# A fused attention and MLP kernel whose instruction order is drawn from another simulation

## The chip, the cores and the metric

The kernel runs on one core of one Trainium2 chip. The metric is the time of one execution on the device, in microseconds (us). Before the change it is 1253.63 us, the median of three runs (1252.76 to 1253.79).

## What is computed

The reference is attention with normalised queries and keys, followed by two MLPs on the 1,792 tokens that come out of it:

```python
q_n, k_n = rmsnorm(q, g_q), rmsnorm(k, g_k)      # q, k, v: 4 x 12 x 448 x 64
attn = softmax(q_n @ k_n.T / 8)
x = (attn @ v), heads side by side               # 1792 x 768
x = (relu(x @ w_in) ** 2) @ w_out                # w_in 768 x 2048, w_out 2048 x 768
out = (((x @ w1) * (x @ w2)) @ w3) @ w_out2      # w1, w2 768 x 1024; w3 1024 x 1024; w_out2 1024 x 768
```

The MLP weights arrive as 64-bit words.

## The kernel before

There are 48 heads (4 batches of 12), and one loop (line 670) goes over them. Every product is made of values split into a high and a low part, so a matmul of the MLPs is three instructions in a row (`mm3`, lines 262 to 264).

**Attention of a head.** `head_prep` makes the scaled keys (`kx`, line 480, then `khl`, lines 108 and 114) and the queries `qh`, `ql`. `stage_k` transposes the keys (line 508). `stage_qk` runs twice per head and makes two score tiles each time (`sc`, lines 524 and 525), whose row maxima VectorE takes (line 526) and scales (line 527, `nb`); `stage_exp` has ScalarE make two tiles `p` from them (line 542). The score tiles have two PSUM buffers, so a pair of scores waits until ScalarE has read the pair before it. `stage_t` transposes `p` (line 564), ScalarE and VectorE split the result (`ptr`, `pte`), and `stage_v` multiplies with the values (line 616); line 605 transposes the sums. Every fourth head `group_prep` makes the norms of four more (lines 450 to 456, and `rsqrt`, lines 428 to 434).

**Fill.** Between the stages of a head, `fill` draws matmuls from a generator, so many for each stage. During heads 0 to 12 it is `gen_w3o`, which multiplies the two last weight matrices with each other (384 matmuls of 384 columns); from then on it is `gen_moe` of the batch that attention has just finished (448 columns). After the last head the MLPs of the last batch run alone.

**Weights.** A weight goes through a chain of units: SyncE loads 64-bit words (`raw64`, line 180, four buffers); ScalarE (line 194) and GpSimd or ScalarE (lines 200, 198) rework the two halves; VectorE joins them (line 207, `raw`, four buffers); ScalarE makes the high part and GpSimd or VectorE the low one (lines 106 and 114, `hl`, four buffers). Units of the first batch are also stored as 32-bit words, which later batches load. The 64-bit units are 120 in all: 32 for `gen_w3o` and 88 for the MLPs of the first batch. The profile's names leave out buffer numbers and write `raw` for `raw64` too, `x`, `act` and `x2` for the split operands of `mm3`.

**Order.** The kernel is traced as one program. When the `TileContext` closes, the framework's scheduler gives each engine its order: it plays the program in a simulation, and each time an engine is free there it takes, among the instructions that the simulation holds ready, the one that was traced first. On the chip each engine then keeps to that order, and semaphores make it wait.

## Time and profile before

| what | before |
|---|---|
| median of three runs | 1253.63 us |
| span of the profiled execution | 1246.1 us |
| TensorE matmul busy | 1173.5 us (94%), 6,192 matmuls |
| VectorE, ScalarE, GpSimd busy | 708.0, 728.9, 780.3 us |
| mean granted TensorE clock | 0.990 |

The span runs from the first to the last instruction. The profile lists no other time of that execution; the median is 7.5 us above its span.

### The profile page before, as it was taken

How to read it: one execution, taken by the hardware profiler on the slowest of the kernel's cores; microseconds unless marked ns; L12 is line 12 of the kernel's file. 1: busy time of each engine (PE TensorE's matmuls, PEld its weight loads, DVE VectorE, ACT ScalarE, POOL GpSimd, SP SyncE). 2: the span in 40 equal slices, each digit the busy share in tenths (PEclk: the TensorE clock that was granted, in tenths of full speed). 3: DMA queues.
4: the chain of work that ended last, by engine and by line, in shares of the span. 5: the costliest groups of instructions: out<-in, count | busy, mean ns of one | idle time of the engine just before them, and what ended most of it. 6: DMA issues, size and time to landing. Idle time of an engine off the chain costs nothing.

```text
span 1246.1 us, 18719 instructions
## 1 busy us (share of the span) xinstructions
PE 1173.5 (94%) x6192; PEld 1060.8 (85%) x6192; DVE 708.0 (57%) x1314; ACT 728.9 (58%) x1553; POOL 780.3 (63%) x772
## 2 busy tenths in 40 slices
PE   3789999898889899999999999999999999999998
PEld 2678888887777788999999999999999999999998
DVE  6699888867887775547567555655664421012110
ACT  5788876756655655566645555656645554443342
POOL 6775435645675665675776664755766556678773
PEclk9999999899999999999999999999999999999999
DMA  7774446876766655344333344332333333433342
GB/s 218 237 225 137 150 140 183 267 215 217 236 205 212 207 158 159 106 117 113 113 102 114 96 130 128 105 105 85 112 95 88 92 114 107 113 108 108 103 121 94
DMA packets 102129, 178.71 MB, mean 143 GB/s; under 512 B 11056, under 2 KB 65552, under 8 KB 102032
## 3 DMA queue, kind: packets, MB, share of 16 engines
q1 hardware_dynamic: 98576, 172.01, 46.6%
q10 hardware_dynamic: 3456, 5.51, 1.2%
q8 instruction: 49, 0.80, 0.3%
q14 instruction: 48, 0.39, 0.1%
HBM read 149.95 MB, written 27.53 MB: 142 GB/s over the span
## 4 chain that ended last, share of the span: by engine, by line
PE 69%; DVE 10%; DMA 7%; ACT 5%; POOL 5%; issue 4%; SPq 0%; ACTq 0%; DVEq 0%; POOLq 0%
PE mm L263 18%; PE mm L262 18%; PE mm L264 18%; PE pt L564 4%; PE kv L616 4%; POOL hl L114 2%; PE sc L524 2%; DMA raw<-w_in 2%; PE sc L525 2%; DVE raw L207 2%; DVE nb L526 2%; ACT p L542 2%; DMA kn<-k_nat 1%; DMA raw<-w 1%; ACT hl L106 1%
## 5 line engine op out<-in xcount | busy, mean ns | idle before, releaser
L114 POOL TENSOR_TENSOR hl<-raw,hl 128x384 fp32r<-128x384 f32 (+1 forms) x383 | 444.6, 1164 | 254.1 <-ACT hl L106 251.2
L106 ACT ACTIVATE hl<-raw 128x384 fp32r<-128x384 f32 (+1 forms) x416 | 233.2, 564 | 149.2 <-PE mm L264 82.2
L263 PE MATMUL mm<-x,hl 128*128 128x448 f32 (+1 forms) x832 | 306.4, 368 | 9.4 <-POOL x L114 9.4
L262 PE MATMUL mm<-x,hl 128*128 128x448 f32 (+1 forms) x832 | 311.0, 374 | 4.0 <-ACT x L106 1.8
L264 PE MATMUL mm<-x,hl 128*128 128x448 f32 (+1 forms) x832 | 305.5, 367 | 0.9 <-POOL hl L114 0.9
L262 PE MATMUL mm<-act,hl 128*128 128x448 f32 (+1 forms) x640 | 238.6, 373 | 0.0
L263 PE MATMUL mm<-act,hl 128*128 128x448 f32 (+1 forms) x640 | 235.8, 368 | 2.2 <-POOL act L114 1.7
L264 PE MATMUL mm<-act,hl 128*128 128x448 f32 (+1 forms) x640 | 234.7, 367 | 1.4 <-POOL hl L114 1.0
L542 ACT ACTIVATE p<-sc,nb,rr 112x448 f32<-112x448 f32 x192 | 137.3, 719 | 75.4 <-DVE nb L527 74.8
L263 PEld LDWEIGHTS mm<-x,hl 128*128 128x128 f32 x832 | 158.2, 190 | 23.2 <-POOL x L114 11.1
L262 PEld LDWEIGHTS mm<-x,hl 128*128 128x128 f32 x832 | 158.1, 190 | 18.9 <-ACT x L106 2.9
L264 PEld LDWEIGHTS mm<-x,hl 128*128 128x128 f32 x832 | 158.2, 190 | 14.9 <-POOL hl L114 2.0
L200 POOL TENSOR_SCALAR raw<-raw 128x384 uint32<-128x384 uint16 (+1 forms) x110 | 87.7, 798 | 84.6 <-DMA raw<-w_in 35.3
L526 DVE TENSOR_REDUCE nb<-sc 112x1 f32<-112x448 f32 x192 | 113.2, 616 | 37.7 <-PE sc L525 36.7
L263 PEld LDWEIGHTS mm<-act,hl 128*128 128x128 f32 x640 | 122.0, 191 | 12.9 <-POOL act L114 3.0
L264 PEld LDWEIGHTS mm<-act,hl 128*128 128x128 f32 x640 | 122.0, 191 | 11.8 <-POOL hl L114 1.8
L262 PEld LDWEIGHTS mm<-act,hl 128*128 128x128 f32 x640 | 122.2, 191 | 9.4 <-ACT act L106 0.2
L114 DVE TENSOR_TENSOR ptr<-pt,ptr 128x448 fp32r<-128x448 f32 x144 | 86.9, 618 | 69.8 <-ACT ptr L106 69.2
L207 DVE SCALAR_TENSOR_TENSOR raw<-raw 128x384 uint32<-128x384 uint32 (+1 forms) x120 | 85.5, 715 | 51.6 <-POOL hl L114 43.5
L564 PE MATMUL pt<-ident,p 112*128 112x112 f32 (+1 forms) x768 | 99.4, 265 | 12.6 <-DVE ptr L114 9.7
L194 ACT ACTIVATE raw<-raw 128x384 f32<-128x384 f32 (+1 forms) x120 | 71.1, 599 | 68.1 <-DMA raw<-w 25.0
L114 POOL TENSOR_TENSOR act<-gf,act 128x448 fp32r<-128x448 f32 x80 | 96.9, 1212 | 8.1 <-ACT act L106 3.2
(80 smaller groups left out, 1542.7 us busy)
## 6 DMA issues: line engine op xcount, KB each, us to landing
raw<-f_in SPq DMA_DIRECT2D x96, 192.0 KB, 2.4
raw<-f_out SPq DMA_DIRECT2D x72, 256.0 KB, 2.6
raw<-f SPq DMA_DIRECT2D x96, 192.0 KB, 2.4
raw<-w_in SPq DMA_DIRECT2D x32, 384.0 KB, 3.5
raw<-w_out SPq DMA_DIRECT2D x24, 512.0 KB, 4.5
raw<-w SPq DMA_DIRECT2D x32, 384.0 KB, 4.0
raw<-w3o SPq DMA_DIRECT2D x48, 256.0 KB, 2.7
qt<-q_t SPq DMA_DIRECT2D x48, 224.0 KB, 2.8
```

The lines of the kernel that those rows point to most:

```text
L106: nc.scalar.activation(out=out, in_=in_, func=AF.Copy)
L114: e.tensor_tensor(out=out, in0=in0, in1=in1, op=ALU.subtract)
L194: nc.scalar.activation(out=hi, in_=hi, func=AF.Prelu, scale=2.0**-112, alpha=-(2.0**32))
L200: nc.gpsimd.tensor_scalar(out=t[:, :n, 0], in0=low, scalar1=2.0**-13, scalar2=2.0**-14 - 0.5, op0=ALU.mult, op1=ALU.add)
L207: nc.vector.scalar_tensor_tensor(out=f[:, :n].bitcast(U32), in0=t[:, :n, 1], scalar=3, in1=t[:, :n, 0], op0=ALU.logical_shift_left, op1=AL ...
L262: nc.tensor.matmul(ps, w[:, 0, wk, :], x[0], start=(i == 0), stop=False)
L263: nc.tensor.matmul(ps, w[:, 0, wk, :], x[1], start=False, stop=False)
L264: nc.tensor.matmul(ps, w[:, 1, wk, :], x[0], start=False, stop=(i == last))
L526: nc.vector.tensor_reduce(out=nb[:, j:j + 1], in_=o[j], axis=AX.X, op=ALU.max, negate=True)
L542: nc.scalar.activation(out=p, in_=o[j], func=AF.Exp, scale=d["rq"][:, c:c + 1], bias=nb[:, j:j + 1], accum_out=sm[:, i, c:c + 1],)
L564: nc.tensor.transpose(ps[:kn, c * P:(c + 1) * P], d["p"][c][:, k0:k0 + kn], ident)
L616: nc.tensor.matmul(ps[:, :S], w, m, start=(n == 0), stop=(n == len(ops) - 1))
```

## The change

The context is told to schedule with the framework's timeline simulation. No instruction is added, removed or resized, and buffers and traced order stay; only the order in which each engine finds its instructions differs, and with it what each waits for.

```diff
-    with tile.TileContext(nc) as tc:
+    with tile.TileContext(nc, schedule_with_timeline_sim=True) as tc:
         attention_moe_kernel(tc, *args)
```

**GpSimd, the very start.** The keys of head 0 (`kx_149`, `khl_151`) and the first unit (`raw64_118`, which becomes `raw_243` and `hl_249`). Before:

```order
L480 TENSOR_TENSOR kx_149<-kn_113,rr_134 112x256
L200 TENSOR_SCALAR raw64_118<-raw64_118 128x512
L108 TENSOR_SCALAR khl_151<-kx_149 112x4x64
L114 TENSOR_TENSOR khl_151<-kx_149,khl_151 112x4x64
L200 TENSOR_SCALAR raw64_122<-raw64_122 128x384
```

Now:

```order
L200 TENSOR_SCALAR raw64_118<-raw64_118 128x512
L480 TENSOR_TENSOR kx_149<-kn_113,rr_134 112x256
L108 TENSOR_SCALAR khl_151<-kx_149 112x4x64
L114 TENSOR_TENSOR hl_249<-raw_243,hl_249 128x512
L114 TENSOR_TENSOR khl_151<-kx_149,khl_151 112x4x64
```

The first unit's work now stands ahead of the keys of head 0, twice. On VectorE the join of that unit (line 207, `raw_243`) likewise stands ahead of the last step of the first `rsqrt`, which `kx_149` needs.

**GpSimd, a little later.** The keys of heads 1 to 3 (`khl_199`, `khl_436`, `khl_651`) and the next units of the fill (`raw64_229` and `raw64_231`, split into `x_260`, `act_269`). Before:

```order
L480 TENSOR_TENSOR kx_197<-kn_113,rr_134 112x256
L108 TENSOR_SCALAR khl_199<-kx_197 112x4x64
L114 TENSOR_TENSOR khl_199<-kx_197,khl_199 112x4x64
L480 TENSOR_TENSOR kx_434<-kn_113,rr_134 112x256
L108 TENSOR_SCALAR khl_436<-kx_434 112x4x64
L114 TENSOR_TENSOR khl_436<-kx_434,khl_436 112x4x64
L480 TENSOR_TENSOR kx_649<-kn_113,rr_134 112x256
L108 TENSOR_SCALAR khl_651<-kx_649 112x4x64
L114 TENSOR_TENSOR khl_651<-kx_649,khl_651 112x4x64
L200 TENSOR_SCALAR raw64_229<-raw64_229 128x384
L200 TENSOR_SCALAR raw64_231<-raw64_231 128x384
```

Now:

```order
L200 TENSOR_SCALAR raw64_229<-raw64_229 128x384
L200 TENSOR_SCALAR raw64_231<-raw64_231 128x384
L114 TENSOR_TENSOR x_260<-raw_247,x_260 128x384
L114 TENSOR_TENSOR act_269<-raw_258,act_269 128x384
L480 TENSOR_TENSOR kx_197<-kn_113,rr_134 112x256
L108 TENSOR_SCALAR khl_199<-kx_197 112x4x64
L114 TENSOR_TENSOR khl_199<-kx_197,khl_199 112x4x64
L480 TENSOR_TENSOR kx_434<-kn_113,rr_134 112x256
L108 TENSOR_SCALAR khl_436<-kx_434 112x4x64
L200 TENSOR_SCALAR raw64_254<-raw64_254 128x384
```

Three heads' keys stood ahead of the units; now the units stand ahead of the keys.

**TensorE, head 10.** The first two scores of head 10 are `sc_1890` and `sc_1894`; `mm_1818` is a tile of `gen_w3o`, and `kv_2004` is the result of head 9. Before:

```order
L524 MATMUL sc_1890<-kt_1781,qh_1711 112x448
L525 MATMUL sc_1890<-kt_1781,ql_1712 112x448
L564 MATMUL pt_1920<-ident_103,p_1831 128x112
L564 MATMUL pt_1927<-ident_103,p_1737 128x112
L564 MATMUL pt_1927<-ident_103,p_1831 128x112
L524 MATMUL sc_1894<-kt_1781,qh_1711 112x448
L525 MATMUL sc_1894<-kt_1781,ql_1712 112x448
L564 MATMUL pt_1920<-ident_103,p_1833 128x112
L564 MATMUL pt_1927<-ident_103,p_1833 128x112
L262 MATMUL mm_1818<-act_319,hl_1591 128x384
L263 MATMUL mm_1818<-act_319,hl_1591 128x384
L264 MATMUL mm_1818<-act_319,hl_1591 128x384
```

Now:

```order
L524 MATMUL sc_1890<-kt_1781,qh_1711 112x448
L525 MATMUL sc_1890<-kt_1781,ql_1712 112x448
L564 MATMUL pt_1920<-ident_103,p_1831 128x112
L564 MATMUL pt_1927<-ident_103,p_1831 128x112
L508 MATMUL kv_1948<-ident_r_104,khl_1878 128x112 x4
L524 MATMUL sc_1894<-kt_1781,qh_1711 112x448
L525 MATMUL sc_1894<-kt_1781,ql_1712 112x448
L564 MATMUL pt_1920<-ident_103,p_1833 128x112
L564 MATMUL pt_1927<-ident_103,p_1833 128x112
L616 MATMUL kv_2004<-ptr_1925,vhl_1767 128x448
L564 MATMUL pt_1955<-ident_103,p_1735 128x112
L564 MATMUL pt_1955<-ident_103,p_1737 128x112
```

The fill has left head 10: there is not one matmul of it from the first score of head 10 to that of head 11, where 24 stood. It went ahead. Counted in the whole order, by the first score of each head (number of fill matmuls issued until then):

| first score of head | 2 | 8 | 13 | 16 | 24 |
|---|---|---|---|---|---|
| fill matmuls, before | 48 | 241 | 388 | 618 | 1263 |
| fill matmuls, now | 34 | 381 | 429 | 625 | 1263 |
| other matmuls, both | 55 | 273 to 277 | 456 to 464 | 569 | 865 |

**TensorE, head 18.** `sc_4067` and `sc_4071` are the first two scores of head 18, `kv_4042` the result of head 16, `mm_3954`, `mm_3955`, `mm_4102` tiles of the MLPs. Before:

```order
L616 MATMUL kv_4042<-ptr_3932,vhl_3581 128x448 x2
L616 MATMUL kv_4042<-pte_3939,vhl_3581 128x448
L524 MATMUL sc_4067<-kt_3925,qh_3786 112x448
L525 MATMUL sc_4067<-kt_3925,ql_3787 112x448
L524 MATMUL sc_4071<-kt_3925,qh_3786 112x448
L525 MATMUL sc_4071<-kt_3925,ql_3787 112x448
L262 MATMUL mm_3955<-act_3704,hl_3963 128x448
L263 MATMUL mm_3955<-act_3704,hl_3963 128x448
```

Now:

```order
L262 MATMUL mm_3955<-act_3877,hl_3963 128x448
L263 MATMUL mm_3955<-act_3877,hl_3963 128x448
L264 MATMUL mm_3955<-act_3877,hl_3963 128x448
L262 MATMUL mm_3955<-act_3949,hl_3963 128x448
L262 MATMUL mm_4102<-act_3417,hl_3997 128x448
L263 MATMUL mm_4102<-act_3417,hl_3997 128x448
L263 MATMUL mm_3954<-act_3949,hl_3914 128x448
L264 MATMUL mm_3954<-act_3949,hl_3914 128x448
L263 MATMUL mm_3955<-act_3949,hl_3963 128x448
L264 MATMUL mm_3955<-act_3949,hl_3963 128x448
L524 MATMUL sc_4067<-kt_3925,qh_3786 112x448
L525 MATMUL sc_4067<-kt_3925,ql_3787 112x448
```

The scores stood right behind `kv_4042`; now 16 fill matmuls stand between them. From head 24 on nearly all instructions keep their places or move by a few.

## Rows read from the trace of the kernel before

**Rows 1.** Busy time by stretch; columns: busy us (instructions) per engine, clock, DMA share, GB/s.

```profile
core 0: us, PE busy (x) PEld busy (x) DVE busy (x) ACT busy (x) POOL busy (x), PEclk, DMA share, GB/s
57.00:132.00 75.00, 67.28 (x413) 60.49 (x412) 69.33 (x133) 65.86 (x139) 48.74 (x56) 1.00 0.59 180
132.00:192.00 60.00, 54.30 (x335) 49.16 (x334) 50.97 (x116) 45.17 (x102) 22.99 (x30) 1.00 0.50 147
192.00:263.00 71.00, 65.85 (x344) 59.31 (x343) 56.13 (x100) 48.31 (x105) 42.58 (x46) 0.95 0.78 231
263.00:490.00 227.00, 202.72 (x1034) 176.55 (x1034) 170.95 (x309) 139.50 (x302) 135.75 (x146) 0.97 0.65 199
490.00:1246.00 756.00, 752.50 (x3973) 692.26 (x3971) 324.97 (x577) 394.25 (x835) 490.74 (x449) 1.00 0.37 108
```

**Rows 2.** Waits of TensorE from 260 to 490: us in total, times, longest.

```profile
PE sc L524 <- ACT p L542: 13.3, 12, 2.7
PE pt L564 <- DVE ptr L114: 5.8, 9, 1.6
```

**Rows 3.** Timeline of GpSimd at the start; columns: start, length.

```profile
6.46 1.01 POOL L480 TENSOR_TENSOR kx<-kn,rr 112x256 f32<-112x256 f32 x1 [5.19 <-DVE rr L434]
7.73 0.64 POOL L200 TENSOR_SCALAR raw<-raw 128x512 uint32<-128x512 uint16 x1 [0.27 <-DMA raw<-w3t]
...
19.74 0.61 POOL L480 TENSOR_TENSOR kx<-kn,rr 112x256 f32<-112x256 f32 x1 [1.11 <-issue]
...
26.34 1.52 POOL L200 TENSOR_SCALAR raw<-raw 128x384 uint32<-128x384 uint16 x2
```

**Rows 4.** Timeline of TensorE: the second and third fill triple.

```profile
26.24 0.69 PE L262 MATMUL mm<-x,hl 128*128 128x384 f32 x1 [1.80 <-ACT x L106]
29.84 0.69 PE L263 MATMUL mm<-x,hl 128*128 128x384 f32 x1 [2.91 <-POOL x L114]
30.32 0.52 PE L264 MATMUL mm<-x,hl 128*128 128x384 f32 x1
30.64 0.52 PE L262 MATMUL mm<-act,hl 128*128 128x384 f32 x1
```

**Rows 5.** Timeline of TensorE: first scores of heads 2, 8, 13 and 16.

```profile
57.05 0.44 PE L524 MATMUL sc<-kt,qh 128*112 128x448 f32 x1
...
132.48 0.46 PE L524 MATMUL sc<-kt,qh 128*112 128x448 f32 x1
...
191.62 0.46 PE L524 MATMUL sc<-kt,qh 128*112 128x448 f32 x1 [1.58 <-ACT p L542]
...
262.74 0.46 PE L524 MATMUL sc<-kt,qh 128*112 128x448 f32 x1 [1.74 <-ACT p L542]
```

**Rows 6.** TensorE unhindered: 384 columns, only 448 columns (stretch), one stage of two heads (chain).

```profile
60.61 0.33 PE L263 MATMUL mm<-x,hl 128*128 128x384 f32 x1
60.78 0.34 PE L264 MATMUL mm<-x,hl 128*128 128x384 f32 x1
...
1150.00:1200.00 50.00, 50.00 (x249) 46.34 (x248) 7.51 (x10) 20.15 (x39) 34.57 (x34) 1.00 0.36 104
...
515.51 0.79 PE pt L564 x8
...
559.96 0.80 PE pt L564 x8
```

**Rows 7.** Shares of the chain of waits, 260 to 340.

```profile
by line: DMA raw<-w_in 18.8%; DMA raw<-w_out 11.9%; issue 7.9%; POOL hl L114 7.5%; DMA kn<-k_nat 6.0%; ACT p L542 5.5%; DVE raw L207 5.3%; DVE nb L526 4.9%; DMA f_in<-raw 3.9%; DVE act L114 3.8%; ACT raw L194 3.5%; ACT hl L106 3.4%; ACT ptr
```

**Rows 8.** Timeline of TensorE around the scores of head 20, and the clock behind them.

```profile
369.18 0.46 PE L524 MATMUL sc<-kt,qh 128*112 128x448 f32 x1 [2.70 <-ACT p L542]
...
371.18 0.57 PE L262 MATMUL mm<-act,hl 128*128 128x448 f32 x1
371.56 0.57 PE L263 MATMUL mm<-act,hl 128*128 128x448 f32 x1
...
370.00:374.00 4.00, 3.70 (x12) 3.31 (x13) 4.00 (x12) 2.23 (x6) 3.02 (x3) 0.61 0.77 232
```

## The prediction, made before the changed kernel was run

> **What bounds the kernel now.** I read the busy time by stretch first. From 490 us to the end TensorE is busy 752.5 of 756 us [rows 1]: there it is the bound, no order of the same matmuls makes it shorter, and only a new wait could make it longer. Up to 490 no engine is full. From 57 to 132 VectorE is busy 92% and TensorE 90%; from 132 to 192 it is 85% and 91%; from 192 on TensorE waits a little everywhere. So the change is decided in the first 490 us, and there by what each in-order engine finds at its head.
>
> Next I read the waits of TensorE and the chain. From 260 to 490 the largest wait is that of the scores for ScalarE's `p`: 13.3 us in 12 times [rows 2]. Behind it stands the weight chain: from 260 to 340 loads of 64-bit units, GpSimd's low parts and VectorE's joins hold much of the chain of waits [rows 7], since `nb` and the joins share VectorE's queue.
>
> Unhindered matmuls give the prices. A 384-column one takes 0.17 to 0.18 us from start to start, 249 of 448 columns take 50 us, so 0.201 each; and two heads took 44.45 us with 168 such fill matmuls and 74 others, so an attention matmul costs (44.45 - 168 x 0.201) / 74 = 0.145 us [rows 6].
>
> **The change, stretch by stretch.** Nothing is added, so each term compares the time between two points that both orders pass, the first scores of heads 2, 8, 13, 16 and 24 (the counts are in the table under the change).
>
> *To head 2: -6 us.* Head 0's keys started on GpSimd at 6.46 and the first unit's words at 7.73 [rows 3]. Now the words come first, and VectorE's join of that unit precedes the norm step that the keys need; words to 8.37, a join and the step put the keys at about 9.2: 2.7 us later. Against that, the keys of heads 1 to 3 held GpSimd from 19.74 to 26.34 ahead of the next units' words [rows 3], and TensorE stood before the second and third fill triple for 1.80 and 2.91 us [rows 4]. These 6.6 us now lie behind the units. And 14 fewer fill matmuls precede head 2, at 0.32 (30.32 to 30.64 [rows 4]) to 0.18 us, say 3.5. Together 2.7 - 6.6 - 3.5 = -7.4; I take -6, because words that come earlier meet loads that may still be landing. Ends: -9 if all gaps close, +3 if only the delay stays.
>
> *Heads 2 to 8: +20 us.* This took 132.48 - 57.05 = 75.4 us [rows 5]; its 193 fill and 218 other matmuls need 193 x 0.177 + 218 x 0.145 = 65.8, so 9.6 were waits. Now 347 fill and 222 others stand there: 61.4 + 32.2 = 93.6 us, however ready everything is. VectorE, with about as much to do as before, has cover to spare, so I add 2 us of waits, not 9.6: 95.6, or +20. Ends: +18 and +28. A scheduler puts fill first when it holds the attention not ready; on the chip the order then has to be kept.
>
> *Heads 8 to 13: -7 us.* This took 191.62 - 132.48 = 59.1 us. The fill has been done ahead, so TensorE now needs only 48 x 0.2 + 187 x 0.145 = 36.7 us and VectorE sets the pace: 50.97 us busy in the 60 from 132 [rows 1], and 105 instructions in place of 112, since four joins went ahead: 47.8. It cannot be under that (-11); if it waits as before, nothing is gained (0). I take 52, nearer to the floor, since most of what it waited for (joins, GpSimd's low parts) has left.
>
> *Heads 13 to 16: -9 us.* This took 262.74 - 191.62 = 71.1 us for 230 fill and 113 other matmuls, which need 62.6. Now 196 and 105 are left, 54.6; at the same ratio 62.0, so -9. Ends: -16 (TensorE never waits) and -2 (the units that were early only wait).
>
> *Heads 16 to 24: -6 us.* The scores of heads 16 to 22 move behind 7 to 14 more instructions. By the order and the prices above the work between a head's last pair of scores and the next head's first grows by 1.0 to 2.8 us, from 6.2 to 7.4 us mostly. Of the waits there (2.70 us at head 20 [rows 8], 13.3 in all [rows 2]) that covers about two thirds, 9 us. Behind the longest, matmuls ran at 0.38 us instead of 0.20 and the granted clock of 370 to 374 was 0.61 [rows 8]; over 263 to 490 it is 0.97 [rows 1], some 7 us lost, and I put 4 of them down to these waits. That is -13 at best. But VectorE answers the scores late because it stands before joins, and the chain shows the units [rows 7]: TensorE freed there will find units missing in part. I take half, -6; ends -13 and +2.
>
> *From head 24 on: 0.* TensorE has no gap to fill [rows 1], and nearly all instructions stand where they stood. The work that hides each small shift is the row of fill matmuls in front; if it ran out, a score's wait of 1 to 2 us per head would return.
>
> Sum: -6 + 20 - 7 - 9 - 6 = -8 us. The profiled span of 1246.1 would become about 1238; with the 7.5 us between span and median, which nothing here touches, 1253.6 - 8 = 1245.6 us.
>
> [...] After a wait of 2.70 us and another short one the granted clock was 0.61, and matmuls took twice as long for about 3 us [rows 8]. [...]
>
> **The rivals.** [...]
>
> *Waits change places (no change).* The scores wait less but the fill waits for units, heads 16 to 24 give 0 and the start gives -4: -4 + 20 - 7 - 9 = 0, 1253.6 us. For it: the unit chain in [rows 7]; against it: TensorE hardly waited for units by name [rows 2].
>
> *All gaps close (faster still).* The start gives -8, heads 16 to 24 -13: -8 + 20 - 7 - 10 - 13 = -18, 1235.6 us.
>
> That the switch does nothing is excluded by the order.
>
> **How the numbers follow.** Forecast 0.44, all gaps 0.16, places 0.13, slower 0.27. About 0.2%, 2.5 us, is what a measurement here can tell from none. So faster 0.60, same 0.13, slower 0.27. The forecast's own range is 1240 to 1251. The whole range runs from a little below the third rival to a little beyond the slower one, whose unknown (heads 8 to 13) could cost some us more: 1233 to 1262.
>
> **What would show it.** In the profile after: head 2's first score before 54 us; heads 2 to 8 in 93 us or more, with TensorE near 100% and VectorE near 70%; heads 8 to 13 in 48 to 55 us, with TensorE near 70%, and its granted clock there deciding between forecast and rival; the waits of scores for `p` between heads 16 and 24 down from 13 us to 5 or less, without waits for `hl` of the same size; from head 24 to the end the same length as before, within 1 us. The prediction is wrong if heads 2 to 8 pass in under 85 us, or if the stretch from head 24 grows.

## The result and the profile after

| what | before | changed |
|---|---|---|
| median on the same chip | 1253.20 us (four runs, 1251.29 to 1253.79) | 1262.21 us (four runs, 1258.67 to 1267.11) |
| ratio, 95% interval | | 1.0077 (1.0057 to 1.0096) |
| span of the profiled execution | 1246.1 us | 1261.7 us |
| mean granted TensorE clock | 0.990 | 0.980 |
| VectorE busy, 1,314 instructions | 708.0 us | 745.3 us |

The changed kernel is slower, by 9.0 us in the medians; the forecast was 8 us faster. Its profiled execution took 1263.43 us, 1.7 above its span, and its three other executions stood 1.7 or 1.8 above theirs. Later runs of the kernel before stood 2.1 to 2.3 above theirs; so its profiled execution took some 1248.3, below its four timed runs. So the stretches below, 15.6 us apart in sum, hold some 6.6 us (15.6 - 9.0) that belong to those two executions and not to the change.

Busy time by stretch in the changed kernel, cut at the first scores of heads 2, 8, 13, 16 and 24 (columns as in [rows 1]: us, busy us and instructions of TensorE, its loads, VectorE, ScalarE and GpSimd, then clock, DMA share, GB/s):

```profile
53.65:156.02 102.37, 97.07 (x571) 90.56 (x570) 69.60 (x129) 73.03 (x157) 57.21 (x66) 0.97 0.57 175
156.02:221.49 65.47, 49.56 (x236) 40.10 (x236) 53.45 (x116) 40.48 (x89) 19.26 (x27) 0.82 0.37 106
221.49:284.59 63.10, 58.37 (x304) 50.94 (x303) 51.05 (x93) 45.21 (x99) 39.80 (x39) 0.97 0.70 224
284.59:485.87 201.28, 180.95 (x935) 158.52 (x935) 164.04 (x286) 126.68 (x277) 129.44 (x136) 0.98 0.71 212
485.87:1261.70 775.83, 770.25 (x4065) 707.01 (x4063) 365.04 (x600) 402.46 (x858) 497.83 (x459) 1.00 0.37 108
```

The same five stretches took 75.4, 59.1, 71.1, 209.1 and 774.3 us before [rows 5]; the last point there is this row of TensorE's timeline of before, the first score of head 24:

```profile
471.82 0.36 PE L524 MATMUL sc<-kt,qh 128*112 128x448 f32 x1
```

The time was lost between heads 2 and 13 (+26.9 and +6.3) and partly won back (-3.4 before head 2, -8.0 and -7.8 after head 13). Two rows stand out: heads 2 to 8, where TensorE is busy 95%, and heads 8 to 13, where it is busy 76% at a clock of 0.82, and VectorE 53.5 us in 116 instructions. By head, 8 to 12, this stretch reads:

```profile
156.02:174.68 18.66, 14.79 (x66) 12.38 (x66) 16.79 (x37) 12.05 (x26) 9.30 (x12) 0.82 0.71 208
174.68:185.79 11.11, 8.19 (x48) 6.67 (x48) 9.02 (x16) 7.87 (x19) 4.49 (x7) 1.00 0.35 97
185.79:195.78 9.99, 6.28 (x36) 4.46 (x36) 7.37 (x17) 5.96 (x15) 2.36 (x4) 0.93 0.11 32
195.78:208.36 12.58, 10.24 (x49) 8.63 (x49) 9.33 (x17) 7.38 (x17) 2.13 (x3) 0.77 0.24 64
208.36:221.49 13.13, 10.05 (x39) 7.96 (x40) 10.95 (x31) 7.22 (x16) 0.99 (x2) 0.62 0.24 66
```

Head 8 alone takes 18.7 us; heads 11 and 12 take 12.6 and 13.1 at 0.77 and 0.62, where head 10 takes 10.0 at 0.93. Inside head 8, the timeline of VectorE, ScalarE, TensorE and SyncE's loads (start, length, in brackets the wait ahead and what ended it):

```profile
155.74 0.33 SPq L405 DMA_DIRECT2D kn<-k_nat  x1
...
155.92 0.17 DVE L547 TENSOR_SCALAR sm<-sm 112x8 f32<-112x8 f32 x1 [3.11 <-ACT p L542]
...
156.02 0.36 PE L524 MATMUL sc<-kt,qh 128*112 128x448 f32 x1
...
159.78 1.06 ACT L450 ACTIVATE qn<-kn 112x1024 f32<-112x1024 f32 x1 [3.48 <-DMA kn<-k_nat]
...
159.89 0.62 DVE L526 TENSOR_REDUCE nb<-sc 112x1 f32<-112x448 f32 x1
160.87 1.22 DVE L452 TENSOR_REDUCE ss<-qn 112x16 f32<-112x1024 f32 x1 [0.36 <-ACT qn L450]
...
162.12 0.33 SPq L406 DMA_DIRECT2D qn<-q_nat  x1
...
166.44 1.06 ACT L450 ACTIVATE qn<-qn 112x1024 f32<-112x1024 f32 x1 [2.17 <-DMA qn<-q_nat]
...
167.81 0.71 ACT L542 ACTIVATE p<-sc,nb,rr 112x448 f32<-112x448 f32 x1
```

The scores stand at 156.02, their exponentials follow at 167.81. Ahead of the exponentials in ScalarE's queue are squares of two later groups (keys of heads 16 to 19, queries of heads 20 to 23), whose loads land late: 3.48 and 2.17 us of waiting. The second load fills the tile that the first square wrote and VectorE summed, so it is issued only behind that sum, at 162.12. Line 547 on VectorE waits for the exponentials of head 7; behind it norm steps of a later group and a join stand ahead of head 8's first maximum (159.89).

The same two squares fell into head 8 before, too (135.92 and 142.61). In the default order with nearly the same fill (the second kernel of the next section) the first also stands ahead of head 8's exponentials with a wait of 0.78, the second behind them, and from score to exponential it is 4.1 us (159.87 to 163.95) in place of 11.8:

```profile
161.30 1.06 ACT L450 ACTIVATE qn<-kn 112x1024 f32<-112x1024 f32 x1 [0.78 <-DMA kn<-k_nat]
...
163.95 0.74 ACT L542 ACTIVATE p<-sc,nb,rr 112x448 f32<-112x448 f32 x1
...
170.59 1.05 ACT L450 ACTIVATE qn<-qn 112x1024 f32<-112x1024 f32 x1
```

The waits of TensorE in heads 16 to 24 answer to [rows 2] (us in total, times, longest):

```profile
PE pt L564 <- DVE ptr L114: 6.2, 8, 1.9
PE sc L524 <- ACT p L542: 6.1, 5, 2.4
PE mm L264 <- POOL hl L114: 5.9, 5, 2.0
```

The waits of scores have halved (13.3 to 6.1), and waits for GpSimd's low parts of weights now stand at 5.9, where this was the row before:

```profile
PE mm L264 <- POOL hl L114: 0.4, 1, 0.4
```

At the start, GpSimd and TensorE answer to [rows 3, 4]:

```profile
7.95 0.65 POOL L200 TENSOR_SCALAR raw<-raw 128x512 uint32<-128x512 uint16 x1 [6.67 <-DMA raw<-w3t]
9.50 0.98 POOL L480 TENSOR_TENSOR kx<-kn,rr 112x256 f32<-112x256 f32 x1 [0.91 <-DVE rr L434]
...
12.18 0.72 POOL L114 TENSOR_TENSOR khl<-kx,khl 112x256 fp32r<-112x256 f32 x1
```

```profile
14.32 0.71 PE L524 MATMUL sc<-kt,qh 128*112 128x448 f32 x1 [0.63 <-ACT kt L106]
...
20.82 0.69 PE L262 MATMUL mm<-x,hl 128*128 128x384 f32 x1 [2.27 <-ACT x L106]
...
30.79 0.73 PE L508 MATMUL kv<-ident_r,khl 112*128 112x112 f32 x4 [3.05 <-POOL khl L114]
```

Head 0's scores start at 14.32 in place of 12.04, and the keys that were put behind the units now cost TensorE a wait of 3.05 us (at 30.79).

### The profile page after: what moved, and what is told of

Read it like the earlier page. It is cut to its first block, busy times and chain, and to the rows that moved or that the text cites. A ratio compares the mean times of both kernels' runs of the same rounds, so it can differ in the third digit from the quotient of the medians.

```text
span 1261.7 us, 18757 instructions
## 1 busy us (share of the span) xinstructions
PE 1180.5 (94%) x6192; PEld 1065.5 (84%) x6192; DVE 745.3 (59%) x1314; ACT 726.3 (58%) x1553; POOL 783.4 (62%) x772
## 4 chain that ended last, share of the span: by engine, by line
PE 59%; DVE 12%; DMA 11%; POOL 6%; ACT 6%; issue 5%; SPq 0%; ACTq 0%; POOLq 0%; DVEq 0%
PE mm L262 16%; PE mm L264 16%; PE mm L263 16%; PE pt L564 3%; DMA raw<-w_in 3%; PE kv L616 3%; DVE raw L207 2%; DMA raw<-w 2%; POOL hl L114 2%; DMA kn<-k_nat 2%; PE sc L524 2%; PE sc L525 2%; DVE nb L526 2%; POOL raw L200 2%; ACT p L542 1%
## 5 line engine op out<-in xcount | busy, mean ns | idle before, releaser
L263 PE MATMUL mm<-act,hl 128*128 128x448 f32 (+1 forms) x640 | 233.5, 365 | 4.0 <-POOL act L114 3.9
L262 PE MATMUL mm<-act,hl 128*128 128x448 f32 (+1 forms) x640 | 235.6, 369 | 1.4 <-ACT hl L106 0.8
L264 PE MATMUL mm<-act,hl 128*128 128x448 f32 (+1 forms) x640 | 232.9, 365 | 1.5 <-POOL hl L114 1.4
L200 POOL TENSOR_SCALAR raw<-raw 128x384 uint32<-128x384 uint16 (+1 forms) x110 | 83.0, 754 | 100.2 <-DMA raw<-w_in 40.8
L526 DVE TENSOR_REDUCE nb<-sc 112x1 f32<-112x448 f32 x192 | 116.2, 616 | 30.0 <-PE sc L525 28.7
L263 PEld LDWEIGHTS mm<-act,hl 128*128 128x128 f32 x640 | 120.8, 189 | 13.8 <-POOL act L114 4.5
L264 PEld LDWEIGHTS mm<-act,hl 128*128 128x128 f32 x640 | 120.6, 189 | 12.0 <-POOL hl L114 2.6
L262 PEld LDWEIGHTS mm<-act,hl 128*128 128x128 f32 x640 | 120.9, 189 | 10.8 <-ACT hl L106 1.2
L564 PE MATMUL pt<-ident,p 112*128 112x112 f32 (+1 forms) x768 | 107.9, 271 | 8.5 <-DVE ptr L114 8.3
L564 PEld LDWEIGHTS pt<-ident,p 112*128 112x128 f32 (+1 forms) x768 | 87.1, 139 | 22.8 <-DVE ptr L114 10.6
```

The lines of the kernel that those rows point to most:

```text
L200: nc.gpsimd.tensor_scalar(out=t[:, :n, 0], in0=low, scalar1=2.0**-13, scalar2=2.0**-14 - 0.5, op0=ALU.mult, op1=ALU.add)
L262: nc.tensor.matmul(ps, w[:, 0, wk, :], x[0], start=(i == 0), stop=False)
L263: nc.tensor.matmul(ps, w[:, 0, wk, :], x[1], start=False, stop=False)
L264: nc.tensor.matmul(ps, w[:, 1, wk, :], x[0], start=False, stop=(i == last))
L526: nc.vector.tensor_reduce(out=nb[:, j:j + 1], in_=o[j], axis=AX.X, op=ALU.max, negate=True)
L564: nc.tensor.transpose(ps[:kn, c * P:(c + 1) * P], d["p"][c][:, k0:k0 + kn], ident)
```

## The experiments

All times are medians beside runs of the kernel before on the same chip; stretches are cut at first scores, as above. Of the sixteen kernels most went another way than expected.

**The fill alone, and the rest alone.** The first kernel keeps the changed scheduling, but on TensorE holds the fill of heads 1 to 12 behind the scores it was traced behind. The second keeps the default scheduling and draws the fill earlier, in nearly the changed kernel's amounts (341 and 40 matmuls in heads 2 to 8 and 8 to 13, where the changed kernel has 347 and 48). Both edits, cut:

```diff
     def fill(n):
+        if state["after"] is not None:   # first kernel: the last score traced, heads 1 to 12
+            with tc.issue_after(state["after"]):
+                draw(n)
+        else:
+            draw(n)
...
         n = W3O / ((H + 1) * 6) if h <= H else MOE / (H * 6)
+        n = AHEAD.get(h, n)   # second kernel
```

> Theory (the fill that runs ahead in heads 2 to 8 is paid there and not given back in heads 8 to 13): with the fill of heads 1 to 12 held behind the scores it was traced behind, heads 2 to 8 fall from 102.4 to 75-80 us, heads 8 to 13 from 65.5 to 58-62, the rest stays as in the changed kernel, and the time is 1236 to 1244 us, some 20 below the changed kernel and 10 below the kernel before. Rival (the loss lies in other moved instructions, of GpSimd, VectorE or the loads): the time stays at 1255 us or more.

> Theory: the kernel before with nothing but its fill moved ahead (48 fill matmuls by head 2, 389 by head 8, 429 by head 13, as in the changed kernel) has the whole loss and none of the gains: heads 2 to 8 take 95 to 102 us, heads 8 to 13 58 to 66 us with a granted clock under 0.9, and the time is 1266 to 1278 us. Rival (the loss lies in other moved instructions): within 5 us of the kernel before, 1248 to 1258.

Measured: 1254.93 us, ratio 1.0020 (1.0007 to 1.0033), and 1258.54 us, ratio 1.0049 (1.0033 to 1.0064). Neither theory holds alone: the two halves cost 0.2% and 0.5%, together about the 0.77% of the change. Stretch by stretch they do not add up: in heads 2 to 8 they cost 10.1 and 27.7 us, the change 26.9; in heads 8 to 13 +9.9 and -7.0, the change +6.3. So the sum of the totals is not shown to be more than chance. Heads 2 to 8 and 8 to 13 of the first, then of the second:

```profile
54.49:139.96 85.47, 76.33 (x426) 68.28 (x425) 67.81 (x121) 64.26 (x137) 49.54 (x57) 0.92 0.51 158
139.96:209.00 69.04, 64.01 (x372) 57.85 (x372) 52.09 (x118) 46.07 (x103) 26.55 (x34) 0.98 0.50 141
```

```profile
56.73:159.87 103.14, 93.53 (x567) 87.30 (x565) 77.82 (x144) 77.37 (x163) 58.05 (x67) 1.00 0.62 182
159.87:211.98 52.11, 42.25 (x228) 33.44 (x228) 46.25 (x104) 38.06 (x86) 16.89 (x25) 0.93 0.40 112
```

With the default order the emptied heads 8 to 13 do take the 52 us that were forecast. But heads 2 to 8 take 103.1, and heads 13 to 16 60.5: +27.7, -7.0 and -10.6 are +10, not the +4 of the forecast for these three. With the fill in its place, the new order takes 10 us more in heads 2 to 8 (ten fill matmuls more explain 1.8 of it; what the rest is, at a clock of 0.92, no run settles) and 10 more in heads 8 to 13 (41 more of them explain 7.3), and wins 2.6 at the start and 10.8 in heads 16 to 24.

**The low clock.** The changed kernel with added matmuls in heads 8 to 12, whose results are overwritten (edit cut):

```diff
         ps = ps_pt.tile([128, 512], F32, name="pt", tag="pt")
+        if 8 <= h + 1 < 13:
+            n = heads[h + 1]
+            with tc.issue_after(n["after"]):
+                for i in range(3):
+                    nc.tensor.matmul(ps[:P, :S], n["qh"][:, :P], n["kt"], start=True, stop=True)
```

> The changed kernel with 60 more matmuls of 448 columns in heads 8 to 12 (12 a head, ahead of the transposes, the head's first score once more into a tile that the transposes then overwrite; 12 us of work at 0.2 each). If the lower clock makes heads 8 to 13 take 65.5 us: the granted clock there is 0.97 or more, the stretch 53 to 58 us, the time 1250 to 1255. Rival (the chain of scores, maxima, exponentials and loads takes 65 us whatever the clock): the stretch takes 65 to 75 us, the time is 1262 to 1270.

Measured: 1264.79 us; heads 8 to 13 63.7 us. Heads 10, 11 and 12 ran at 1.00 and took 31.3 us in place of 35.7, though 7.2 us of work was added to them; head 8 took 20.2 (18.7) and head 9 12.3 (11.1). So the clock is a cause in the last heads, but not that of head 8, and the sum did not fall: 1.0094 times the kernel before (1.0074 to 1.0113), where the change has 1.0077. Heads 10 to 12 in one row:

```profile
191.80:223.08 31.28, 27.19 (x156) 21.69 (x157) 27.03 (x64) 20.94 (x47) 7.25 (x11) 1.00 0.24 65
```

**Where the later gain comes from.** The first kernel again, with the fill of all heads held behind the scores, so that the scores of heads 13 to 24 stand early, as before the change; and the kernel before, with the scores of heads 13 to 23 traced behind the first draw of fill:

```diff
+        if 13 <= h < 24:
+            fill(n)
         stage_qk(h, 0)
-        fill(n)
+        if not 13 <= h < 24:
+            fill(n)
```

> As the first run, but the fill of all heads is held behind the scores, so that in heads 13 to 24 too the scores stand where they stood before the change (618 fill matmuls by head 16, 702 by head 17). Theory (scores behind more fill are worth what the changed kernel gained there): heads 16 to 24 take about 209 us in place of 201.3, and the time is 6 to 8 us above the first run's, 1243 to 1250. Rival (that gain came from units that were made earlier, not from the place of the scores): the same as the first run within 2 us.

> The kernel before with its own scheduling; only in heads 13 to 23 the first of the six draws of fill is traced ahead of the head's first scores in place of behind them (633 fill matmuls by head 16, 714 by head 17, where 618 and 702 stood). Theory (the changed kernel's gain in heads 16 to 24 is the place of the scores and nothing else): heads 16 to 24 take 198 to 203 us in place of 209, all else as before, the time 1240 to 1247 us, 6 to 10 us below the kernel before. Rival (the gain needs the new order of the other engines): within 3 us of the kernel before.

Measured: 1262.65 us and 1256.21 us (ratio 1.0024, 1.0010 to 1.0038). Heads 16 to 24 took:

| | default order | new order |
|---|---|---|
| scores early | 209.1 (before) | 206.9 (fill of all heads held) |
| scores behind fill | 212.6 (scores moved alone) | 198.3 (first kernel), 201.3 (the change) |

The first expectation came true (+8.6 over 198.3), the second did not: the move alone gains nothing. Its waits of TensorE show what took the place, then two waits of VectorE in heads 16 to 24, of before and of the changed kernel:

```profile
PE pt L564 <- DVE ptr L114: 14.7, 8, 3.9
PE mm L264 <- POOL hl L114: 6.7, 7, 2.9
PE mm L262 <- ACT hl L106: 2.4, 3, 1.1
PE sc L524 <- ACT p L542: 1.0, 2, 0.7
```

```profile
DVE raw L207 <- POOL hl L114: 30.9, 22, 3.6
```

```profile
DVE raw L207 <- POOL hl L114: 17.2, 13, 3.6
```

The scores' wait is gone (13.3 to 1.0), and the transposes' (5.8 to 14.7) and the weights' (under 0.5 to 6.7) took its place. In the new order VectorE stands before joins for 17.2 us in place of 30.9 (34.9 with the scores moved alone); only there does a late score pay. With the scores early in the new order TensorE waited 15.4 us for them, while VectorE's wait was 18.7. That it is this wait of VectorE that decides, and nothing else of the new order, is argued from these rows and not tested by itself.

**Orders joined at one head.** Here each engine's order is written out: instructions traced before a head in one kernel's order, the others behind them in the other's.

```diff
         attention_moe_kernel(tc, *args)
+        keep_order(tc, nc)   # each instruction queued behind the one ahead of it in a table
```

> Each engine's order is written out: what was traced before head 13 in the order of the kernel before, the rest in the changed kernel's order. Theory (the change loses before head 13 and gains from there on, and the gain does not need the loss): up to head 13 as before (about 192 us), heads 16 to 24 in 198 to 202 us in place of 209, the time 6 to 11 us below the kernel before, 1241 to 1247 us. Rival (the gain is only work moved ahead in the early heads): heads 16 to 24 take 206 us or more and the time is within 3 us of the kernel before.

> The other way round: what was traced before head 13 in the changed kernel's order, the rest in the order of the kernel before; 388 fill matmuls stand ahead of head 13, as before the change. Theory: the whole loss and none of the gain: heads 2 to 8 take about 102 us, heads 8 to 13 58 to 65, heads 13 to 16 about 71, heads 16 to 24 about 209; the time is 1272 to 1282 us. Rival (the loss lies in the later heads or in work that crosses head 13): within 6 us of the changed kernel, 1256 to 1268.

> As the first of these four, but what was traced before head 2 also in the changed kernel's order (units ahead of the keys of heads 1 to 3). Theory (the start was worth 3.4 us there): head 3 starts 2 to 4 us earlier than before and the time is 1 to 4 us below the first of these four. Rival (the early gain was only 14 fill matmuls put off): the same time within 1 us.

> As the run with the order of the kernel before up to head 13 and the changed kernel's from there, with the seam at head 16, in the middle of a batch's matmuls. Theory (the new order of all engines gains in heads 16 to 24 whatever came before): heads 0 to 16 take 262 to 268 us, heads 16 to 24 198 to 203 in place of 209, and the time is 2 to 10 us below the kernel before. Rival (the gain needs units that the new order had made ahead before head 16): heads 16 to 24 take 206 us or more, or the seam costs 8 us or more in heads 15 to 17, and the time is that of the kernel before or longer.

Measured: 1268.73, 1299.51, 1272.16 and 1257.57 us, all longer than expected, because of the seam: nothing traced behind it can run ahead of it, loads and units included. Head 12 of the first (36.3 us in place of 11.8; head 13 took 36.4 in place of 19.4) and head 16 of the last (42.5 in place of 27.1):

```profile
176.63:212.97 36.34, 22.66 (x111) 19.94 (x112) 17.05 (x31) 17.77 (x36) 11.16 (x13) 0.81 0.51 151
```

```profile
259.78:302.32 42.54, 26.36 (x122) 22.94 (x121) 24.44 (x47) 19.68 (x38) 15.68 (x21) 0.80 0.53 159
```

Away from the seam the stretches answer. Heads 16 to 24 took 199.0 in the first, where the heads before 12 passed as before: the gain needs no loss in the heads before 12. In the second they took 209.7, and heads 2 to 8 102.3: the loss stays without the gain. In the last, heads 17 to 24 took 177.8, where before took 182.0 and the changed kernel 174.3. The third shows nothing of the start, whose seam cost 13 us.

**Head 8.** In the changed kernel's order, written out, the two squares move behind the exponentials of heads 8 and 9; in another kernel the 45 MLP matmuls that ran ahead into heads 8 to 12 are held; a third does both.

```diff
-L450 ACTIVATE qn<-kn 112x1024          (ScalarE: ahead of the exponentials of head 8)
 L542 ACTIVATE p,sm<-sc,nb,rr 112x448 x2
+L450 ACTIVATE qn<-kn 112x1024
```

> The changed kernel's order written out, with ScalarE's two squares of later groups that stand at the first scores of head 8 moved behind the exponentials of heads 8 and 9, VectorE's sums of them likewise, and the load that fills the second one's buffer. Theory (ScalarE stands there before loads that have not landed, 3.48 and 2.17 us, and the exponentials of head 8 behind them): head 8 takes 11 to 14 us in place of 18.7, heads 8 to 13 57 to 60 in place of 65.5, and the time is 5 to 8 us below the changed kernel, 1254 to 1257 us. Rival (the low clock of TensorE sets that stretch): heads 8 to 13 take 63 us or more and the time is 1260 to 1264.

> The changed kernel's schedule with the matmuls of the MLPs that run ahead into heads 8 to 12 (45 of 448 columns) held behind the scores of head 13; up to head 8 nothing moves, and 384 fill matmuls stand ahead of head 13 in place of 429. Theory (head 8 is long because TensorE, VectorE and ScalarE stand there before units of the MLPs whose loads have not landed): head 8 takes 10 to 13 us in place of 18.7, heads 11 and 12 stay at 12 to 14 us with the low clock, heads 8 to 13 take 55 to 59 us in place of 65.5; the 45 matmuls come back in heads 13 to 16, 69 to 73 us in place of 63.1; the time is within 4 us of the changed kernel. Rival (that work is not what holds head 8): head 8 takes 17 us or more and the time is 1266 us or more.

> The order of the run with the MLP matmuls held behind head 13, written out, with ScalarE's two squares of later groups moved from the scores of head 8 to behind the exponentials of heads 8 and 10, VectorE's sums of them and one load likewise. Theory (there ScalarE stands 3.5 and 1.2 us before these loads, VectorE 2.0 us for the squares, and head 8's exponentials behind them): head 8 takes 10 to 13 us in place of 17.5, heads 8 to 13 57 to 61 in place of 65.5, the time is 4 to 9 us below that run's 1277.0. Rival (another wait takes their place, or the low clock eats it): heads 8 to 13 take 63 us or more, the time is within 3 us of 1277.

Measured: 1268.01, 1277.01 and 1282.44 us. The squares' theory fell twice. In the first, head 8 took 17.4 us and head 9 18.5; in ScalarE's queue the next load in line took the squares' place:

```profile
165.87 0.57 ACT L194 ACTIVATE raw<-raw 128x384 f32<-128x384 f32 x1 [4.00 <-DMA raw<-w_in]
...
167.15 0.70 ACT L542 ACTIVATE p<-sc,nb,rr 112x448 f32<-112x448 f32 x1
```

These are words of an MLP unit whose load had not landed. In the second, head 8 took 17.5; in the third 16.4, and head 11, which got the second square, 16.3. What shortens head 8 is taking all later work out of the queues at once: in the kernel that joins the orders at head 13 (the changed kernel's first) it took 9.8. That takes the later loads and GpSimd's work away as well (DMA share 0.13 in the rows below, where it was 0.32), so it does not tell the place in the queues from the load on the DMA engines.

**Both causes.** The kernel with the MLP matmuls held, with the added matmuls of the clock's experiment; and those matmuls with everything traced from head 13 on held on every engine:

> As the run before, with 60 more matmuls of 448 columns in heads 8 to 12 (12 a head, the head's first score once more into a tile that the transposes then overwrite). Theory (with only attention left the low clock is worth 2 to 4 us a head there): the granted clock of heads 8 to 13 is 0.97 or more and they take 48 to 53 us, some 6 us less than without the added matmuls, though those are 12 us of work. Rival (the clock is a symptom): as long as without them or longer.

> The changed kernel's order with the 60 added matmuls in heads 8 to 12 (12 us of work), written out, and all that was traced from head 13 on queued behind all that was traced before, on every engine. Theory (low clock and later work in the queues are the two causes): heads 8 to 13 take 46 to 51 us, where they took 56.3 with the later work away alone and 63.7 with the matmuls added alone; the seam costs in heads 13 to 16 as it did before, so the whole is 1280 us or more. Rival (something else holds the stretch): 54 us or more.

Measured: 1265.63 us, 11.4 below the same kernel without them (1277.01), and 1289.28 us. The second's seam lies in head 12, so the stretch to compare ends at head 12's first score. Windows of heads 8 to 11 in six kernels: the changed kernel; the same with added matmuls; MLP held; MLP held with added matmuls; all later work held; all later work held with added matmuls.

```profile
156.02:208.36 52.34, 39.50 (x198) 32.14 (x197) 42.51 (x86) 33.26 (x74) 18.28 (x25) 0.87 0.41 116
```

```profile
159.39:211.78 52.39, 45.54 (x242) 36.96 (x242) 39.62 (x87) 33.04 (x74) 18.19 (x26) 0.93 0.39 111
```

```profile
159.21:211.93 52.72, 34.12 (x152) 25.93 (x150) 38.33 (x82) 31.16 (x68) 14.08 (x20) 0.75 0.32 85
```

```profile
159.85:206.02 46.17, 36.41 (x197) 28.86 (x196) 36.09 (x79) 29.61 (x67) 13.75 (x20) 0.89 0.32 84
```

```profile
157.25:199.60 42.35, 31.59 (x153) 23.05 (x151) 31.77 (x67) 25.80 (x61) 9.93 (x15) 0.83 0.13 36
```

```profile
155.31:192.14 36.83, 32.71 (x196) 26.39 (x196) 28.98 (x63) 25.58 (x59) 10.17 (x15) 1.00 0.14 40
```

In the changed kernel itself the added matmuls gain nothing in these four heads (52.4 against 52.3), where the clock stood at 0.87. With the MLP matmuls held it fell to 0.75; there they gain 6.5 us, and with all later work held 5.5. Taking the later work away gains 10.4 and 9.3, and VectorE has 67 instructions in place of 82 or 86. Together that is 15.9 of 52.7. In these kernels the two causes add, and the four heads, which took 52.3 in the changed kernel, need 36.8 without them and without the MLP matmuls, whose removal alone changed nothing (52.7).

**The clock elsewhere.** The same added matmuls, four a head, in the kernel before (heads 13 to 23) and in the first kernel (heads 2 to 23):

> The kernel before, all else in its order, with 44 more matmuls of 448 columns in heads 13 to 23 (4 a head, one ahead of each set of transposes, the head's first score once more; 8.8 us of work). If they fall into TensorE's waits and hold its clock: the granted clock of heads 13 to 24 rises from 0.95 and 0.97 to 0.99 or more and the time is 1 to 5 us below the kernel before, 1247 to 1251 us. Rival (they stand in the way of scores and transposes): 2 to 9 us above it.

> The first run's kernel (fill of heads 1 to 12 held behind its scores), with 88 more matmuls in heads 2 to 23 (4 a head, 17.6 us of work). If they hold the clock: the granted clock of heads 2 to 8 rises from 0.92 to 0.98 or more, that stretch falls from 85.5 to 78-82 us, and the time is 3 to 9 us below that run, 1246 to 1252 us. Rival: the same time or up to 10 us longer.

Measured: 1262.67 and 1286.35 us, 10.7 above the kernel before and 31 above the first kernel. Where fill stands in every head the added work only stood in the way: in the first, heads 13 to 16 ran at 1.00 in place of 0.95 and yet took 74.3 us in place of 71.1; in the second, heads 2 to 8 took 99.3 us in place of 85.5, at a clock of 0.90. No kernel of the sixteen beat the kernel before.

## Why the prediction was wrong

| term | predicted | measured |
|---|---|---|
| to head 2 | -6 | -3.4 |
| heads 2 to 8 | +20 | +26.9 |
| heads 8 to 13 | -7 | +6.3 |
| heads 13 to 16 | -9 | -8.0 |
| heads 16 to 24 | -6 | -7.8 |
| from head 24 | 0 | +1.5 |
| sum | -8 | +15.6 (medians: +9.0) |

- **The step that failed is "I take 52, nearer to the floor, since most of what it waited for (joins, GpSimd's low parts) has left."** It took 65.5. The prediction gave a slower time 0.27, with these heads as its unknown, and the 1262.2 measured stands at the upper end of its range. That a lower clock through all five heads would make them longer was an estimate that no run shows: the clock was 0.82, 1.00, 0.93, 0.77 and 0.62 from head 8 to head 12, and it is only part of what they cost. 52 was right for the shift as such: the default order with nearly the same fill took 52.1. Two things came on top in the new order. One is the clock: the granted one fell to 0.62 in head 12, and 49.6 us of TensorE's busy time stand against the 36.7 reckoned. Not all of these 13 us are the clock: in the default order TensorE was busy 42.3 us there at 0.93. What lowers the clock no run shows: heads 11 and 12, at 0.77 and 0.62, had TensorE busy 81% and 77% of their time, while heads 9 and 10, where it was busy 74% and 63%, kept 1.00 and 0.93. Adding matmuls, which brought the clock back to 1.00 in heads 10 to 12 of the changed kernel, gained 4.4 us there, and 5.5 to 6.5 in heads 8 to 11 where the MLP matmuls were held (clock from 0.83 to 1.00, and from 0.75 to 0.89). The other cause I had not seen: the stretch is not emptied on the other engines. VectorE ran 116 instructions in 53.5 us, where I counted 105 and a floor of 47.8, and the default order with nearly the same fill ran 104 in 46.3. Squares, unit words and joins stand ahead of the exponentials, some before loads in flight (waits of 3.48 and 2.17 us). Taking all later work away was worth 9 to 10 us, some 8 of them in head 8. I read TensorE's order at head 10 and inferred that what stood in the other queues had left too.
- **Heads 2 to 8 were mis-sized: "so I add 2 us of waits, not 9.6".** The count held: 93.6 us of work. Waits were 5.3 (102.37 - 97.07) and slow matmuls 3.5 (97.07 - 93.6; the granted clock was 0.97). In the default order with that fill TensorE stood idle for 9.6 us (103.14 - 93.53), before for 7.7 (75.00 - 67.28 [rows 1]). VectorE's spare time did not shorten the waits there.
- **The start was half right.** Head 0's keys started 3.0 us later (9.50 against 6.46; 2.7 forecast) and its scores 2.3, but the keys put behind the units made a new wait of 3.05 us. The -3.4 measured is no more than the 3.5 that the 14 fill matmuls put off were reckoned at.
- **Heads 13 to 16 and 16 to 24 came as forecast**, -8.0 and -7.8. For the second the reason was incomplete: scores behind fill gained only in the new order, where VectorE also stood less before joins (17.2 us in place of 30.9). My sign that waits for `hl` would not grow was wrong (5.9 us).
- **From head 24** +1.5 in place of 0. In the five profiles whose end is in the default order this stretch took 774.3 to 775.4 us, in the thirteen in the new order 774.7 to 776.5, 1.2 apart in the medians: a small loss. The prediction had named such growth as a sign of being wrong; what makes it was not tested.
- **"the 7.5 us between span and median, which nothing here touches"** was no fixed part: an execution stands 1.7 to 2.3 us above its span, and the profiled one of before was short.

What stays open: which of the later instructions in head 8 costs how much, and how much of it is the loads' share of the DMA engines. Single ones moved away gave their wait to the next, and only all of them together were shown to count. Why the simulation puts them there was not tried.

## What to carry to other kernels

Count what a reordering moves on every engine's queue, not on the busiest alone: matmuls moved out of a stretch shortened it less while the other engines' queues still held later work (heads 8 to 11 took 52.7 us with the MLP matmuls held, 42.4 with all later work held). Fill moved ahead was paid where TensorE became the busiest (95% in heads 2 to 8), and it came back only in part: 17.6 of 27.7 us in the default order, and less in the new one, where the clock also fell in the heads that it had left (0.82). Ending one wait gained little where the next in line was not ready (head 8 took 17.4 us in place of 18.7): test moves singly and together before adding them up.

## What the runs showed of the hardware

Added matmuls shortened one kernel: 12 us of work whose results are thrown away took 11.4 us off the time (1277.01 to 1265.63) where TensorE had only attention left. Of the same kind, 8.8 us of work cost 10.7 us where TensorE had fill, and in the changed kernel itself, where MLP matmuls ran in head 8, it gained nothing (1.0094 times the kernel before, against 1.0077 without them).

VectorE's 37 us more of busy time come with the same instructions. Line 493 (`qh`) takes 0.44 us at its shortest and did so in most of its 36 times before; in the changed kernel twenty of them took longer, up to 4.5 us. The two lines show its groups, before and then changed:

```profile
L493 DVE TENSOR_SCALAR qh<-qt,gg 128x448 fp32r<-128x448 f32 x36 | 18.4, 510 | 0.0
```

```profile
L493 DVE TENSOR_SCALAR qh<-qt,gg 128x448 fp32r<-128x448 f32 x36 | 37.3, 1036 | 0.2 <-PE sc L524 0.2
```

One of the long ones, in the timeline of the changed kernel beside GpSimd's:

```profile
531.85 2.25 POOL L114 TENSOR_TENSOR act<-gf,act 128x448 fp32r<-128x448 f32 x2
...
532.90 3.40 DVE L493 TENSOR_SCALAR qh<-qt,gg 128x448 fp32r<-128x448 f32 x1
...
534.07 1.99 POOL L114 TENSOR_TENSOR hl<-raw,hl 128x384 fp32r<-128x384 f32 x2
```

It ends at 536.30, just behind GpSimd's four instructions in a row (536.06); each of the twenty ends 0.24 to 0.26 us behind the end of a GpSimd instruction, as do the seven long ones of before. Why they end together was not tested. From head 24 on, where this one lies, TensorE was busy 770.25 of 775.83 us, and the stretch grew by 1.5 us in all; in head 8 a norm step of 0.19 us (line 433) took 1.63 (156.44 to 158.07) beside a GpSimd instruction that ended at 158.01, ahead of the scores' maxima.
